# Local attention with two gated layers: a new order of the attention's instructions on each engine, and block means as three halves

## The chip, the cores and the metric

One core of a Trainium2 chip runs the whole program. The metric is the time of the program on the device in microseconds; three runs give a median, and one more run is profiled. TensorE is called PE here (PEld its weight loads), VectorE DVE, ScalarE ACT, GpSimd POOL, and SyncE SP, which issues all of this kernel's DMAs.

## The reference

Attention over 2 x 8 heads, 768 positions, head size 64. Each query sees the keys within 15 positions of it and, beside them, one summary for each of 24 blocks of 32 positions: the block's element-wise maximum of k and its mean of v. Two gated layers follow.

```
k_sum = k.reshape(B, H, nb, block, D).max(axis=3)
v_sum = v.reshape(B, H, nb, block, D).mean(axis=3)
scores_l = where(|pos_i - pos_j| < 16, scale * q k^T, -1e9)
scores_s = scale * einsum('bhsd,bhnd->bhsn', q, k_sum) + log(block)
a = exp(concat([scores_l, scores_s]) - max);  a = a / (sum(a) + 1e-9)
x = concat([v, v_sum]) weighted by a, heads side by side      # 1536 x 512
h = x @ w_in;   x = (h * cos(h)) @ w_out                      # d_ff 2048
h = x @ w_in2;  out = (h * tanh(softplus(h))) @ w_out2
```

## The kernel before

**Attention.** Heads are handled in 8 pairs, queries of a pair in 3 chunks of 256 positions (4 sub-blocks of 64), so there are NS = 24 chunks. The loop at L511 runs i = 0 to 28, and each pass ("turn") works on several chunks at different stages: scores and softmax of chunk i, transposes of the probabilities of chunk i-2 (`probsT`), their product with v of chunk i-3 (`pv`), and the split of the result of chunk i-4 into a high and a low part, `xh` and `xl` (`evac`), which are the layers' input. A turn also prepares later pairs: `prep_k` transposes k on PE, ACT copies it to `KX` (`ev`), DVE takes the block maxima `ks` (`kmax`), and POOL writes these into gaps of `KX` (`prep_ks`); `prep_q` transposes q, DVE scales it into `qt` (`qev`), POOL copies it into `QB` (`qbd`).

One sub-block's keys stand in one window of 118 rows or columns: 15 of the neighbour, 12 block summaries, 64 own, 12 block summaries, 15 of the other neighbour. `VW` holds these windows for v, three buffers, used in turn by the pairs. The block means of v in it come from two sources. For pairs 0 to 2, `prep_vm` multiplies `VW` by the constant `means` on PE (24 instructions) and ACT copies the result to `vm`. For pairs 3 to 7, `load_vb` loads the last 10 heads of v in two groups of 5 into one buffer `vb` (120 partitions of 8 KB), `block_sums` adds them up on POOL in 9 steps, and the means are `VS` (`vs`). `prep_vs` then spreads `vm` (4 DMAs) or `vs` (8 DMAs) over `VW`.

**Order of the work.** It is written out by hand. A phase name is given to each instruction by `at`; `flush` emits them phase by phase in the order of `ORDER` (L262), and each engine works through its own instructions strictly in that order. DMAs of `load`, `load_v` and `load_vb` are issued when the turn's plan is gone through, so ahead of all phases; those of `prep_vs` are in phase `misc`, at the end. SP's queue is in order as well: an issue that must wait for a buffer holds all that follow. Before, a turn's order is: on PE scores (L427 to L432), transposes of `pn`, preparing transposes, product with v; on DVE `mx` (L433), `qt`, the two instructions for `rs` (L441, L442), `xl`, `ks`; on ACT exponentials (L435), `xh`, `kx` and `vm`, `pt`; on POOL `pn` (L444), the copies to `QB`, the gaps of `KX`, the block sums.

**The first layer's weights.** They come as 64-bit numbers and are narrowed in place: `wnarrow` has one step on ACT (L131) and three on DVE (L135, L138, L141); `wsplit` makes a high part on ACT (L149) and a low part on POOL or DVE (L152). Chunks 0 to 3 are done in the attention by `filler(i)` (L524), which runs after all phases of turn i; it also has PE begin the first layer (`up`) at turns 24 to 26.

**Layers.** From L527 on: matrix products with operands split in high and low parts, gates on ACT and DVE, the narrowing of later weights on DVE. Nothing of them is changed.

Of the kernel before, what the change touches and what calls it, by code (L numbers as in the profile page):

```python
# [21 lines left out]
def kernel(  # L22
# [175 lines left out]
    def attention(filler):  # L198
        with ExitStack() as es:
# [11 lines left out]
            means = p1.tile([EXT, NSUB, NB], F32, tag="means", name="means")  # L211
# [37 lines left out]
            def build_means():  # L249

                nc.gpsimd.memset(means, 1.0 / BLK)
                for pattern, base, step in (
                    ([[SUB, NSUB], [-BLK, NB]], -SIDE, 1), ([[-SUB, NSUB], [BLK, NB]], SIDE + BLK - 1, -1),
                    ([[0, NSUB], [0, NB]], -SIDE, 1), ([[0, NSUB], [0, NB]], SIDE + SUB - 1, -1),
                ):
# [6 lines left out]
            ORDER = ("sc", "max", "exp", "tp", "tr", "qev", "rec", "norm", "xh", "xl", "ev", "pth", "kmax", "pv", "qbd", "misc")  # L262
# [38 lines left out]
            def block_sums(g, c):  # L301
# [4 lines left out]
                at("misc", nc.gpsimd.tensor_tensor, out=x[:, r:r + n, :], in0=x[:, r:r + n, :],  # L306
                   in1=x[:, r + w:r + w + n, :], op=ALU.add)
                if c == 8:
                    at("misc", nc.gpsimd.tensor_scalar, out=VS[g], in0=x[:, 0, :], scalar1=1.0 / BLK, scalar2=None,
                       op0=ALU.mult)  # L310

            def prep_vm(n):

                ps = BANK[4][0:NB, 256:384]
                for s in range(NSUB):
                    at("tr", nc.tensor.matmul, ps, lhsT=means[:, s, :], rhs=VW[n % 3][:, s], start=(s == 0),
                       stop=(s == NSUB - 1))
                vm = VM[n] = p2.tile([NB, 2, D], F32, tag="vm", name="vm")
                at("ev", nc.scalar.copy, vm.rearrange("p e d -> p (e d)"), ps)

            def prep_vs(n):

                for h in range(2):
                    for r0, s0 in ((HALO, h), (SIDE + SUB, 1 - h)):
                        dst = VW[n % 3][r0:r0 + GAP, s0:NSUB:2]
                        if 2 * n < MADE:
                            src = VM[n][GAP * h:GAP * h + GAP].rearrange("p e d -> p (e d)")
                            at("misc", nc.sync.dma_start, out=dst.rearrange("p s e d -> p s (e d)"),
                               in_=src[:, None, :].to_broadcast([GAP, NSUB // 2, 2 * D]))
                            continue  # L330
                        for e in range(2):
                            i = 2 * n + e - MADE
                            x0 = NB * (i % HPG) + GAP * h
                            at("misc", nc.sync.dma_start, out=dst[:, :, e, :],
                               in_=VS[i // HPG][x0:x0 + GAP, None, :].to_broadcast([GAP, NSUB // 2, D]))
# [7 lines left out]
            def prep_ks(n):  # L343
# [4 lines left out]
                for h in range(2):  # L348
                    at("misc", eng.tensor_copy, x[:, h:NSUB:2, 0:GAP],
                       ks[:, None, GAP * h:GAP * h + GAP].to_broadcast([128, NSUB // 2, GAP]))  # L350
                at("misc", eng.tensor_copy, KX[n % 2][:, HALO + NSUB * PITCH:HALO + NSUB * PITCH + GAP],
# [51 lines left out]
            for n in range(1, NP):  # L403
                if 2 * n < MADE:
                    plan(3 * n + 1, prep_vm, n)
                plan(3 * n + 2 if 2 * n < MADE else 3 * n, prep_vs, n)
                if n > 2:
                    plan(3 * n - 3, load_v, n)
            for g in range(2):
                plan((2, 7)[g], load_vb, g)  # L410
                for c in range(9):
                    plan((4, 10)[g] + c // 2, block_sums, g, c)
# [63 lines left out]
            wz = p1.tile([128, 512], BF16, tag="wz", name="wz")  # L476
            nc.vector.memset(wz, 0.0)

            def warm(m, bank):
                for _ in range(m):  # L480
# [468 lines left out]
```

## Time and profile before

| | us |
|---|---|
| median of 3 runs (lowest, highest) | 676.29 (675.84, 678.15) |
| profiled execution | 674.55 |
| its span, first to last instruction | 672.6 |
| PE busy, share of the span | 621.8, 92% |
| DVE busy | 503.1, 75% |
| ACT busy | 333.7, 50% |
| POOL busy | 87.0, 13% |

The span holds two parts. The attention takes the first 150 us or so, and there all engines are partly idle; in the layers PE is close to always busy. Busy shares over the whole span therefore say little of the attention: it has to be read by stretches, and in it turn by turn. A row of a timeline gives the start, the duration and, in brackets, how long the engine had been idle before it and which instruction ended that.

### The profile page before, as it was taken

The page shows a single profiled execution, that of the slowest core. Times are in us where ns is not written, and L with a number is a line of the kernel's source. Part 1 is how long each engine was busy: PE and PEld are TensorE (multiplying, and loading weights), DVE is VectorE, ACT ScalarE, POOL GpSimd, SP SyncE. Part 2 cuts the span into 40 slices and gives each one's busy share as a digit, 9 for nine tenths or more (in the row PEclk, how much of TensorE's full clock was granted, in tenths as well). Part 3 has the DMA queues.
Part 4 walks back from the last instruction along what each step waited for, and adds up shares of the span by engine and source line. Part 5 has one row for each costly group of instructions (what it writes and reads, how often), then busy time and mean ns, then how long its engine had stood idle before and what let it go on. Part 6 is the DMA issues. An engine that isn't in the chain of part 4 may idle for free.

```text
span 672.6 us, 8404 instructions
## 1 busy us (share of the span) xinstructions
PE 621.8 (92%) x2971; PEld 517.9 (77%) x2972; DVE 503.1 (75%) x879; ACT 333.7 (50%) x730; POOL 87.0 (13%) x160
## 2 busy tenths in 40 slices
PE   8782877788799999999999999999999999999998
PEld 5682766766588888888888888888888888888886
DVE  4453466639968898888888996887888888888654
ACT  3463366647655564444444555566343534444330
POOL 6373475410000000000000124000000000000000
PEclk9897879788899999999999999999999999999999
DMA  9856864101312231121121110021212121121004
GB/s 189 152 106 133 148 152 97 47 1 62 95 62 88 92 104 63 62 64 62 63 62 64 64 62 1 9 94 54 95 32 94 33 93 63 63 71 55 0 17 172
DMA packets 61207, 51.17 MB, mean 76 GB/s; under 512 B 48158, under 2 KB 49278, under 8 KB 60926
## 3 DMA queue, kind: packets, MB, share of 16 engines
q1 hardware_dynamic: 61166, 50.65, 28.4%
q8 instruction: 23, 0.38, 0.2%
q14 instruction: 18, 0.15, 0.1%
HBM read 46.31 MB, written 3.15 MB: 74 GB/s over the span
## 4 chain that ended last, share of the span: by engine, by line
PE 79%; ACT 7%; DVE 7%; POOL 2%; issue 2%; DMA 1%; SPq 0%; ACTq 0%; POOLq 0%; DVEq 0%
PE bank L706 19%; PE bank L577 19%; PE bank L691 18%; PE bank L188 18%; PE bank L266 5%; ACT pb L266 4%; DVE mx L266 2%; ACT xh L266 1%; DMA kn<-in_k_dram 1%; DVE wx L138 1%; ACT pt L266 1%; ACT kx L266 1%; DVE r L555 1%; DVE r L554 1%; DVE ks L266 1%
## 5 line engine op out<-in xcount | busy, mean ns | idle before, releaser
L188 PE MATMUL bank<-xh,ws 128*128 128x512 f32 x384 | 129.4, 399 | 2.0 <-DVE gg L561 1.9
L577 PE MATMUL bank<-gh,ws 128*128 128x512 f32 x384 | 126.3, 391 | 4.3 <-ACT ws L149 3.1
L706 PE MATMUL bank<-ws,gh 128*128 128x512 f32 (+1 forms) x388 | 118.5, 387 | 0.0
L691 PE MATMUL bank<-xh,ws 128*128 128x512 f32 x272 | 91.0, 389 | 0.0
L188 PEld LDWEIGHTS bank<-xh,ws 128*128 128x128 f32 x384 | 74.4, 194 | 18.5 <-DVE gg L561 2.8
L577 PEld LDWEIGHTS bank<-gh,ws 128*128 128x128 f32 x384 | 72.2, 188 | 20.6 <-ACT ws L149 3.7
L706 PEld LDWEIGHTS bank<-ws,gh 128*128 128x128 f32 x388 | 72.6, 188 | 14.9
L188 PE MATMUL bank<-xl,ws 128*128 128x512 f32 x192 | 76.6, 399 | 0.0
L553 ACT ACTIVATE n<-bank,b_quarter 128x512 int32<-128x512 f32 x48 | 32.9, 686 | 86.3 <-PE bank L188 86.3
L706 PE MATMUL bank<-ws,gl 128*128 128x512 f32 (+1 forms) x194 | 75.0, 387 | 0.0
L577 PE MATMUL bank<-gl,ws 128*128 128x512 f32 x192 | 74.7, 389 | 0.0
L149 ACT CAST ws<-wx 128x512 fp32r<-128x512 f32 x64 | 39.6, 620 | 51.5 <-DVE wx L141 51.5
L266 ACT ACTIVATE pb<-bank,mx 128x118 f32<-128x118 f32 x96 | 33.2, 358 | 55.6 <-DVE mx L266 49.6
L691 PEld LDWEIGHTS bank<-xh,ws 128*128 128x128 f32 x272 | 51.1, 188 | 10.6
L662 DVE TENSOR_TENSOR gl<-gg,gh 128x512 fp32r<-128x512 f32 x48 | 34.0, 708 | 30.2 <-ACT gh L661 30.2
L718 DVE TENSOR_TENSOR acc<-acc,bank 128x512 f32<-128x512 f32 (+1 forms) x71 | 47.5, 674 | 8.5 <-PE bank L706 8.5
L691 PE MATMUL bank<-xl,ws 128*128 128x512 f32 x136 | 52.9, 389 | 0.0
L554 DVE SCALAR_TENSOR_TENSOR r<-n,bank 128x512 f32<-128x512 int32 x48 | 32.9, 685 | 26.2 <-ACT n L553 26.1
L592 POOL TENSOR_TENSOR xl<-acc,xh 128x512 fp32r<-128x512 f32 x10 | 14.6, 1474 | 263.1 <-ACT xh L590 263.1
L266 PE MATMUL bank<-pt,vw 118*128 118x128 f32 x192 | 30.0, 306 | 18.3 <-DMA vw<-in_v_dram 12.7
L138 DVE SCALAR_TENSOR_TENSOR wx<-wst,wx 128x512 int32<-128x512 int32 x64 | 45.1, 705 | 2.2
L141 DVE SCALAR_TENSOR_TENSOR wx<-wst,wx 128x512 int32<-128x512 int32 x64 | 44.6, 697 | 1.8
(109 smaller groups left out, 1064.6 us busy)
## 6 DMA issues: line engine op xcount, KB each, us to landing
wst<-in_moe_w_in_dram SPq DMA_DIRECT2D x32, 512.0 KB
wst<-in_moe_w_out_dram SPq DMA_DIRECT2D x32, 512.0 KB
kn<-in_k_dram SPq DMA_DIRECT2D x16, 192.0 KB
qn<-in_q_dram SPq DMA_DIRECT2D x16, 192.0 KB
vw<-in_v_dram SPq DMA_DIRECT2D x16, 192.0 KB
out_dram<-acc SPq DMA_DIRECT2D x11, 256.0 KB
vb<-in_v_dram SPq DMA_DIRECT2D x2, 960.0 KB
vw<-in_v_dram SPq DMA_DIRECT2D x32, 41.2 KB
```

What stands on the lines that cost most here:

```text
L138: nc.vector.scalar_tensor_tensor(out=xi, in0=word[:, :, 0], scalar=29, in1=xi, op0=ALU.logical_shift_right, op1=ALU.bitwise_or)
L141: nc.vector.scalar_tensor_tensor(out=xi, in0=word[:, :, 1], scalar=-2 ** 31, in1=xi, op0=ALU.bitwise_and, op1=ALU.bitwise_or)
L149: nc.scalar.copy(hi, x)
L188: nc.tensor.matmul(ps, lhsT=SLOT[4 * (g % 2) + a][:, 512 * c + 128 * f:512 * c + 128 * f + 128], rhs=X[e][:, c, TB * j:TB * j + TB], start ...
L266: todo[phase].append(lambda: fn(*a, **kw))
L553: nc.scalar.activation(out=n, in_=h, func=AF.Identity, scale=1.0 / TWO_PI, bias=b_quarter)
L554: nc.vector.scalar_tensor_tensor(out=r, in0=n, scalar=-C1, in1=h, op0=ALU.mult, op1=ALU.add)
L577: nc.tensor.matmul(ps, lhsT=x, rhs=y, start=(n == 0), stop=(n == len(mm) - 1))
L662: later.append(lambda: nc.vector.tensor_tensor(out=lo, in0=g, in1=hi.bitcast(F32), op=ALU.subtract))
L691: nc.tensor.matmul(ps, lhsT=u, rhs=v, start=start and n == 0, stop=stop and n == len(mm) - 1)
L706: nc.tensor.matmul(ps, lhsT=x, rhs=y, start=(n == 0 and (h == 0 or not stay)), stop=(n == len(mm) - 1 and (h == NH - 1 or not stay)))
L718: nc.vector.tensor_tensor(out=acc, in0=acc, in1=ps, op=ALU.add)
```

## The change

`ORDER` is replaced: three new phases (`sums` for the block sums, `fill` for the weight work and `up`, `gap` for the gaps of `KX`) and another sequence. By engine, a turn is now: PE scores, preparing transposes (with the products for `vm`), transposes of `pn`, product with v, `up`; DVE `mx`, `qt`, weight steps, `ks`, `rs`, `xl`; ACT `xh`, `kx` and `vm`, `pt`, weight steps, exponentials; POOL block sums, weight halves, copies to `QB`, `pn`, gaps. `softmax`, which makes `rs` and `pn`, is called for chunk i-1 instead of i. `vm` becomes 12 partitions by three halves (first, second, first again), so that one DMA spreads two neighbouring halves over a row of windows: `prep_vs` has two DMAs a pair. For pairs 3 to 7, `vm` is now filled in turn 3n by four small DMAs from `vs` and a copy on POOL, and `prep_vs` follows in turn 3n+1. `means` holds 6 sub-blocks by 12 instead of 12 by 24 columns. The second `vb` load goes from turn 7 to 9 and its sums from 10 to 11 on; weight chunks 2 to 5 load one or two turns later. The warm-up products of PE have 256 columns, and there are twice as many.

```diff
-            ORDER = ("sc", "max", "exp", "tp", "tr", "qev", "rec", "norm", "xh", "xl", "ev", "pth", "kmax", "pv", "qbd", "misc")
+            ORDER = ("sc", "xh", "sums", "max", "tr", "tp", "ev", "qev", "pv", "pth", "fill", "qbd", "kmax", "rec", "exp",
+                     "xl", "norm", "gap", "misc")
...
             def prep_vm(n):
-                ps = BANK[4][0:NB, 256:384]
-                for s in range(NSUB):
-                    at("tr", nc.tensor.matmul, ps, lhsT=means[:, s, :], rhs=VW[n % 3][:, s], start=(s == 0),
-                       stop=(s == NSUB - 1))
-                vm = VM[n] = p2.tile([NB, 2, D], F32, tag="vm", name="vm")
-                at("ev", nc.scalar.copy, vm.rearrange("p e d -> p (e d)"), ps)
+                vm = VM[n] = p2.tile([GAP, 3, 2, D], F32, tag="vm", name="vm")
+                if 2 * n >= MADE:
+                    for e in range(2):
+                        i = 2 * n + e - MADE
+                        src = VS[i // HPG][NB * (i % HPG):NB * (i % HPG) + NB]
+                        for h in range(2):
+                            at("misc", nc.sync.dma_start, out=vm[:, h, e, :], in_=src[GAP * h:GAP * h + GAP])
+                    at("misc", nc.gpsimd.tensor_copy, vm[:, 2], vm[:, 0])
+                    return
+                for h in range(2):
+                    ps = BANK[4][0:GAP, 256 + 128 * h:384 + 128 * h]
+                    for s in range(NSUB // 2):
+                        at("tr", nc.tensor.matmul, ps, lhsT=means[:, s, :], rhs=VW[n % 3][:, NSUB // 2 * h + s],
+                           start=(s == 0), stop=(s == NSUB // 2 - 1))
+                ps = BANK[4][0:GAP, 256:512].rearrange("p (h e d) -> p h e d", h=2, e=2)
+                at("ev", nc.scalar.copy, vm[:, 0:2], ps)
+                at("ev", nc.scalar.copy, vm[:, 2], ps[:, 0])
 
             def prep_vs(n):
-
-                for h in range(2):
-                    for r0, s0 in ((HALO, h), (SIDE + SUB, 1 - h)):
-                        dst = VW[n % 3][r0:r0 + GAP, s0:NSUB:2]
-                        if 2 * n < MADE:
-                            src = VM[n][GAP * h:GAP * h + GAP].rearrange("p e d -> p (e d)")
-                            at("misc", nc.sync.dma_start, out=dst.rearrange("p s e d -> p s (e d)"),
-                               in_=src[:, None, :].to_broadcast([GAP, NSUB // 2, 2 * D]))
-                            continue
-                        for e in range(2):
-                            i = 2 * n + e - MADE
-                            x0 = NB * (i % HPG) + GAP * h
-                            at("misc", nc.sync.dma_start, out=dst[:, :, e, :],
-                               in_=VS[i // HPG][x0:x0 + GAP, None, :].to_broadcast([GAP, NSUB // 2, D]))
+                for h, r0 in ((0, HALO), (1, SIDE + SUB)):
+                    at("misc", nc.sync.dma_start,
+                       out=VW[n % 3][r0:r0 + GAP].rearrange("p (s h) e d -> p s (h e d)", h=2),
+                       in_=VM[n][:, h:h + 2].rearrange("p h e d -> p (h e d)")[:, None, :].to_broadcast(
+                           [GAP, NSUB // 2, 4 * D]))
...
             for n in range(1, NP):
-                if 2 * n < MADE:
-                    plan(3 * n + 1, prep_vm, n)
-                plan(3 * n + 2 if 2 * n < MADE else 3 * n, prep_vs, n)
+                plan(3 * n + 1 if 2 * n < MADE else 3 * n, prep_vm, n)
+                plan(3 * n + 2 if 2 * n < MADE else 3 * n + 1, prep_vs, n)
...
             for g in range(2):
-                plan((2, 7)[g], load_vb, g)
+                plan((2, 9)[g], load_vb, g)
                 for c in range(9):
-                    plan((4, 10)[g] + c // 2, block_sums, g, c)
+                    plan((4, 11)[g] + c // 2, block_sums, g, c)
...
                 if i < NS:
                     scores(i)
-                    softmax(i)
+                if 1 <= i < NS + 1:
+                    softmax(i - 1)
...
+                at("fill", filler, i)
                 flush()
-                filler(i)
...
-    for c, (t0, t1) in enumerate(((7, 10), (9, 12), (12, 15), (14, 17))):
+    for c, (t0, t1) in enumerate(((7, 10), (9, 12), (13, 16), (15, 18))):
...
-    at_step(17, wload, 0, 0, 4)
-    at_step(19, wload, 0, 0, 5)
+    at_step(19, wload, 0, 0, 4)
+    at_step(21, wload, 0, 0, 5)
```

In `block_sums` the phase is `sums` in place of `misc`, in `prep_ks` it is `gap`.

## Rows read from the trace of the kernel before

**Rows 1.** Busy time by stretch: us, busy (x count) by engine, clock, DMA share, GB/s.

```profile
40.00:52.50 12.50, 10.77 (x92) 9.75 (x91) 7.35 (x19) 7.77 (x33) 9.62 (x18) 1.00 0.37 79
56.40:68.40 12.00, 0.01 (x1) 0.04 (x1) 1.61 (x5) 2.37 (x10) 1.72 (x4) 0.64 1.01 206
86.00:94.00 8.00, 6.30 (x29) 5.98 (x30) 5.44 (x13) 5.20 (x17) 6.58 (x10) 0.57 0.31 67
152.70:176.30 23.60, 17.34 (x64) 12.45 (x62) 23.12 (x39) 15.97 (x26) 0.00 (x0) 0.92 0.28 89
176.30:672.60 496.30, 492.96 (x2173) 408.16 (x2173) 404.67 (x651) 237.29 (x398) 14.58 (x10) 1.00 0.20 64
```

**Rows 2.** SP's waits, up to 140 us: us in total, times, longest.

```profile
SPq L299 <- POOL vs L266: 12.3, 1, 12.3
```

**Rows 3.** Timeline of turn 9, SP and PE: start, us, instruction.

```profile
58.80 4.92 SPq L266 DMA_DIRECT2D vw<-vm  x4
68.39 2.05 PE L266 MATMUL bank<-pt,vw 118*128 118x128 f32 x8 [12.72 <-DMA vw<-in_v_dram]
```

**Rows 4.** Timeline of one turn without weight work, DVE and ACT.

```profile
41.38 0.64 DVE L266 TENSOR_REDUCE mx<-bank 128x4 f32<-128x472 f32 x1
42.11 0.36 ACT L266 ACTIVATE pb<-bank,mx 128x118 f32<-128x118 f32 x1 [1.11 <-DVE mx L266]
43.62 0.17 DVE L266 TENSOR_SCALAR rs<-sm 128x4 f32<-128x4 f32 x1 [1.27 <-ACT pb L266]
44.24 0.86 DVE L266 TENSOR_TENSOR xl<-bank,xh 64x256 fp32r<-64x256 f32 x2 [0.24 <-ACT xh L266]
44.50 0.59 ACT L266 COPY pt<-bank 118x512 f32<-118x512 f32 x1
45.47 0.64 DVE L266 TENSOR_REDUCE mx<-bank 128x4 f32<-128x472 f32 x1
```

**Rows 5.** Timeline, PE: the first instruction of turns 8 and 9.

```profile
49.70 0.36 PE L266 MATMUL bank<-mask,msel 67*128 67x472 bf16 x1
52.56 0.36 PE L266 MATMUL bank<-mask,msel 67*128 67x472 bf16 x1
```

**Rows 6.** Weight chunks in the attention: xcount, ns shortest/median/longest, first and last start.

```profile
L131 ACT ACTIVATE wx<-wst x4: 671/680/691, 76.2 to 113.4; 128x512 f32<-128x512 f32 x4
L135 DVE TENSOR_SCALAR wx<-wx x4: 427/672/1345, 76.9 to 114.1; 128x512 int32<-128x512 int32 x4
L138 DVE SCALAR_TENSOR_TENSOR wx<-wst,wx x4: 892/893/894, 81.5 to 119.6; 128x512 int32<-128x512 int32 x4
L141 DVE SCALAR_TENSOR_TENSOR wx<-wst,wx x4: 691/692/1099, 82.5 to 120.5; 128x512 int32<-128x512 int32 x4
L152 POOL TENSOR_TENSOR ws<-wx,ws x4: 1257/1268/1270, 89.7 to 126.2; 128x512 fp32r<-128x512 f32 x4
```

**Rows 7.** Timeline, PE: the scores of turn 3.

```profile
25.65 2.03 PE L266 MATMUL bank<-kx,qb 128*128 128x118 f32 x8 [4.18 <-POOL kx L266]
```

**Rows 8.** Timeline of SP's issues: v of one pair, then its means.

```profile
109.88 0.66 SPq L288 DMA_DIRECT2D vw<-in_v_dram  x1
113.54 6.68 SPq L266 DMA_DIRECT2D vw<-vs  x8
```

**Rows 9.** POOL's instructions, columns as in rows 6.

```profile
L266 POOL COPY qb<-qt x42: 388/396/549, 20.2 to 129.4; 64x256 f32<-64x256 f32 x42
L266 POOL TENSOR_TENSOR pn<-pb,rs x24: 971/972/974, 12.8 to 139.5; 128x472 f32<-128x472 f32 x24
L266 POOL TENSOR_TENSOR vb<-vb x18: 318/722/1173, 36.7 to 99.4; 120x256 f32<-120x256 f32 x14, 120x128 f32<-120x128 f32 x2, 120x64 f32<-120x64 f32 x2
```

**Rows 10.** Timeline of the attention's end, PE and DVE.

```profile
137.75 0.60 PE L266 MATMUL bank<-ident,pn 128*118 128x128 f32 x4
140.50 1.14 PE L266 MATMUL bank<-pt,vw 118*128 118x128 f32 x8 [2.15 <-ACT pt L266]
152.67 0.69 DVE L554 SCALAR_TENSOR_TENSOR r<-n,bank 128x512 f32<-128x512 int32 x1
```

More of the change, by code (lines that the diff above doesn't have):

```diff
@@ L210, in attention @@
             mask = p1.tile([MROWS, 6, EXT], BF16, tag="mask", name="mask")
-            means = p1.tile([EXT, NSUB, NB], F32, tag="means", name="means")
+            means = p1.tile([EXT, NSUB // 2, GAP], F32, tag="means", name="means")
             def build_mask():
@@ L252, in build_means @@
                 for pattern, base, step in (
-                    ([[SUB, NSUB], [-BLK, NB]], -SIDE, 1), ([[-SUB, NSUB], [BLK, NB]], SIDE + BLK - 1, -1),
-                    ([[0, NSUB], [0, NB]], -SIDE, 1), ([[0, NSUB], [0, NB]], SIDE + SUB - 1, -1),
+                    ([[SUB, NSUB // 2], [-BLK, GAP]], -SIDE, 1), ([[-SUB, NSUB // 2], [BLK, GAP]], SIDE + BLK - 1, -1),
+                    ([[0, NSUB // 2], [0, GAP]], -SIDE, 1), ([[0, NSUB // 2], [0, GAP]], SIDE + SUB - 1, -1),
                 ):
@@ L305, in block_sums @@
                            (0, 2, 2), (0, 1, 1))[c]
-                at("misc", nc.gpsimd.tensor_tensor, out=x[:, r:r + n, :], in0=x[:, r:r + n, :],
+                at("sums", nc.gpsimd.tensor_tensor, out=x[:, r:r + n, :], in0=x[:, r:r + n, :],
                    in1=x[:, r + w:r + w + n, :], op=ALU.add)
                 if c == 8:
-                    at("misc", nc.gpsimd.tensor_scalar, out=VS[g], in0=x[:, 0, :], scalar1=1.0 / BLK, scalar2=None,
+                    at("sums", nc.gpsimd.tensor_scalar, out=VS[g], in0=x[:, 0, :], scalar1=1.0 / BLK, scalar2=None,
@@ L348, in prep_ks @@
                 for h in range(2):
-                    at("misc", eng.tensor_copy, x[:, h:NSUB:2, 0:GAP],
+                    at("gap", eng.tensor_copy, x[:, h:NSUB:2, 0:GAP],
                        ks[:, None, GAP * h:GAP * h + GAP].to_broadcast([128, NSUB // 2, GAP]))
-                at("misc", eng.tensor_copy, KX[n % 2][:, HALO + NSUB * PITCH:HALO + NSUB * PITCH + GAP],
+                at("gap", eng.tensor_copy, KX[n % 2][:, HALO + NSUB * PITCH:HALO + NSUB * PITCH + GAP],
                    ks[:, 0:GAP])
@@ L475, in attention @@
             load(0, "q")
-            wz = p1.tile([128, 512], BF16, tag="wz", name="wz")
+            wz = p1.tile([128, 256], BF16, tag="wz", name="wz")
             nc.vector.memset(wz, 0.0)
             def warm(m, bank):
-                for _ in range(m):
-                    at("sc", nc.tensor.matmul, BANK[bank], lhsT=wz[:, 0:128], rhs=wz, start=True, stop=True)
+                for n in range(2 * m):
+                    at("sc", nc.tensor.matmul, BANK[bank][:, 256 * (n % 2):256 * (n % 2) + 256], lhsT=wz[:, 0:128], rhs=wz,
+                       start=True, stop=True)
             make_identity(nc, ident)
```

## Prediction

> **What bounds the kernel now.** I read first the stretches of busy time and clock [rows 1], then the waits, then single turns in the order of time. "Turn i" is pass i of the attention loop; PE starts it with the scores of chunk i. Three marks cut the execution: PE begins the scores of turn 9 at 52.56 us [rows 5], the transposes of turn 24 at 137.75, and VectorE (DVE) its first instruction of the layers at 152.67 [rows 10]. So A, up to turn 9, is 52.56; B, turns 9 to 23, 85.19; C, the attention's tail, 14.92; D, the layers, 672.6 - 152.67 = 519.93. Around the span lie 674.55 - 672.6 = 1.95 us; the median of the runs is 1.74 above the profiled one.
>
> In D, VectorE is busy 23.12 of the first 23.60 us, and PE 492.96 of the 496.30 after them [rows 1]. Nothing of that is changed, so D moves as a block: what A to C lose, the kernel loses.
>
> B has two faults. The first is one stall. The second load of `vb` is issued at turn 7 but must wait 12.3 us on SP's queue until GpSimd (POOL) has made the first `vs` [rows 2], which it does last in its turn. Behind it stand the copies of pair 2's means, issued only from 58.80; PE's product of turn 9 waits 12.72 us, until 68.39 [rows 3]. The second is the length of a turn. In a turn without weight work [rows 4] ScalarE (ACT) waits 1.11 us for the row maxima `mx`. From one `mx` to the next, 4.09 us, VectorE sits in front of the row sums' reciprocal for 1.27 us until the exponentials are done, then 0.24 us for `xh`, and only after both halves of `xl` and a block maximum comes the next `mx`, on which the next exponentials hang. VectorE's own work is 4.09 - 1.27 - 0.24 = 2.58; ACT's runs without a break from 42.11 to the end of `pt` at 45.09, 2.98; PE's turn at the full clock is 52.56 - 49.70 = 2.86 [rows 5]. None of the three needs 4.09.
>
> **The change part by part.** *Reciprocals a turn later, `mx` first after the scores, `xl` last.* The reciprocal now asks for exponentials that ended a turn ago, and the exponentials, last on ACT, ask for an `mx` that VectorE made early. The ring between VectorE and ACT opens, and the largest of 2.58, 2.98 and 2.86 sets the turn. With one handover of 0.24, the one seen before `xl`, I take 3.2 for a turn without weight work. Seven of B's turns are such (9, 14, 15, 20 to 23): 22.4.
>
> *Weight work inside the turn.* Each of four chunks takes two turns of VectorE (10 and 11, 12 and 13, 16 and 17, 18 and 19): 2 x 2.58, plus the three steps at medians of 0.67, 0.89 and 0.69, plus 0.68 in which the first step waits for ScalarE's part [rows 6]. Behind that wait stand now `kmax`, the reciprocals and `xl`, where before it stood at the end of the turn. That is 8.1 a pair, 32.4 for four. B without more is 54.8.
>
> *The `vb` load at turn 9, the sums first on POOL.* SP's 12.3 us go: turn 8 has finished `vs` by then, and pair 2's copies no longer stand behind the load. But what was late there is late elsewhere. At turn 9 SP issues q of pair 5, v of pair 4, then `vb` (120 x 8 KB, 0.98 MB), a weight chunk (0.52 MB), and only then the four new small copies `vs` to `vm`. Six issues of v take 113.54 - 109.88 = 3.66 us [rows 8], and can start only when pair 1's last product has freed its buffer, at the end of turn 8. Then 1.5 MB at 206 GB/s, the rate of the stretch in which the first stall sat [rows 1], are 7.3 us. After their last byte comes the landing: nothing shows a small copy alone; it is between 0 and the 4.67 us from the end of issue at 63.72 to 68.39 [rows 3], nearer the low end since that row had a queue in front, so 1. The copies land about 12 us after turn 9 begins.
>
> Who waits: the last POOL instruction of turn 9 copies half of `vm` and waits for them. On POOL stand behind it turn 10's q copies (0.40 each, two) and its product `pn` (0.97) [rows 9], which end at 13.8. PE wants this `pn` in turn 11, at 3.2 + 4.05 + 1.7 (scores and preparing transposes of that turn) = 8.95. So PE stands 4.9 us. Afterwards POOL lags: turns 11 to 14 carry two sums each (0.72), two q copies, `pn`, and twice a weight half (1.27) [rows 6, 9], about 4.5 at the most against VectorE's 4.05; I add 1 for it and 1 for the same copy at turn 15, where a weight chunk again precedes it. Together 7, bounds 0 (all landed early) and 15 (a landing at 17, all sums at their longest, 1.17).
>
> The Trainium skill, *DMA: Bandwidth & Descriptors*, section on the anatomy of one DMA, gives a fixed cost of about 2.0 us per DMA, mostly the write receipt, for the GpSimd path; it speaks against a path of two copies in a row. No row here shows a small copy alone. Taken here, the landing would be 2 instead of 1 and the sum 1 us more.
> The same skill, *GPSIMD Engine Reference*, section 1, says POOL shares its SBUF interfaces with VectorE when the latter has two SBUF inputs or a two-port mode. A denser VectorE would then lengthen the sums; the row's spread up to 1.17 agrees, and the bound above holds it.
>
> *Clock.* In 40 to 52.5 us PE had 1.0 granted with 10.77 of 12.5 busy; in the 12 us of idleness it fell (mean 0.64), and in 86 to 94, with 6.30 of 8 busy at the slower pace, it was 0.57 [rows 1]. The new turns leave PE as little idle time as the first of these; the 4.9 us stall may drop the clock for one or two turns. I add 1 (0 to 3). B is 54.8 + 7 + 1 = 62.8, against 85.19: -22.4.
>
> *Means as halves, two DMAs a pair.* A pair's eight copies cost SP 6.68 us of issue [rows 8]; two of the same kind, at 1.23 each (4.92 for four [rows 3]), and four small ones at no more than 0.84 (6.68 / 8) are 5.8. SP is not the bound in B; its relief is counted at nothing. If it were, it would be under 1 us a pair. For pairs 0 to 2 the products with `means` stay 24 instructions, now ahead of the transposes: nothing.
>
> *A.* In turn 2, PE waits 4.18 us for POOL's part of `kx` [rows 7], which came after the q copies and the turn's own `pn`. Now `pn` is that of the turn before and the reciprocal no longer stands between; half goes, -2. The plain turns 3, 5, 6 and 8 and the smaller `means` table: -1. Bounds 0 and -4.
>
> *C.* PE's product waits 2.15 us for `pt` [rows 10], since ACT copies it behind `xh`, behind the exponentials of the same turn. Now the exponentials are last: -2, bounds 0 and -4. *Warm-up in 256 columns, later weight chunks*: the same columns, and chunk 3 still done at turn 20 before the layers need it at 24; nothing, and a turn if the loads were late.
>
> **The sum.** A 49.6, B 62.8, C 12.9, D 519.9: 645.2, plus 1.95, is 647.1 for the profiled execution, -27.4. With 1.74, the median is 648.8.
>
> **The rivals.** *R1, the stall only moves.* The copy behind `vb` lands at 17 rather than 12, and the sums take 1.17: B +8, 657. For it: DMA engines are fully taken in such a stretch (share 1.01) [rows 1]. *R2, POOL never waits*: the small copies slip through; B -8, 641. *R3, the order buys nothing*: another ring keeps the turn where it is, and only the SP wait goes; A and C stay and B loses 12.72 less the 4.9 at turn 11: 676.3 - 7.8 = 668.5. Against it: no ring in the new order needs an answer within the same turn but `mx` to exponentials. *R4, PE at the lower level throughout B*: twice 2.86 in 15 turns is 85.8, so only A's and C's part is left: 676.3 - 5 + 0.6, 672. The stretch at 86 to 94 speaks for it, the one at 40 to 52.5 against.
> *R5, slower: every pair's copy on POOL waits, not the first alone.* The place is the last POOL instruction of turns 9, 12, 15, 18 and 21; `pn` follows 1.8 after the landing, PE needs some 1.5 for the rest of its turn, so a pair takes L + 3.3 where L is the landing. Five pairs equal before (85.19 and the 5 from A and C) at L = 14.7; at L = 17, B is 101.5 and the kernel 676.3 + 16.3 - 5 = 687.6. Against it: only turn 9 has 1.5 MB in front; the others have v and at most one chunk.
>
> **How the numbers follow.** Forecast 0.54 (642 to 655), R1 0.18, R2 0.12, R3 0.07, R4 0.04, R5 0.05. Low end 636: R2 with A and C at their best. High end 665: B at +15 with A or C at nothing; it leaves out R3 to R5, 0.16, and a little at the low side. 0.3% (2 us) is about what can be told from no change. Faster: all but R5 and a part of R4, 0.94; same 0.01; slower 0.05.
>
> **What would show it.** SP's wait before `vb` gone; `mx` no longer behind `xl` and reciprocals free of waits; turns near 3.2 without and 4.05 with weight work; about 5 us of PE idle near turn 11, ended by POOL's `pn`, with a DMA wait on POOL before it; the stretch from the first layer instruction to the end still 520. It is wrong if turns stay at 4.1, if PE's clock stays low through B, or if POOL waits for DMA in every pair.

## The result, and the profile after

The changed kernel takes 655.17 us (653.64 to 655.38); beside it on the same chip the kernel before took 676.07 (675.36 to 678.15). The ratio is 0.968, with a 95% interval of 0.966 to 0.971. So it is faster, by about 21 us. The forecast was 648.8, 27.5 less than the median shown of before, with a range of 636 to 665.

The changed kernel cut at the same four marks (scores of turn 9, transposes of turn 24, first layer instruction on DVE), columns as in [rows 1]: busy us and count of PE, PE's loads, DVE, ACT, POOL, then clock, DMA share, GB/s.

```profile
0.00:48.76 48.76, 42.09 (x344) 36.70 (x345) 24.63 (x67) 27.39 (x108) 29.19 (x82) 1.00 0.92 177
48.76:121.75 72.99, 52.57 (x364) 48.72 (x361) 44.88 (x114) 47.71 (x191) 41.91 (x73) 0.84 0.54 119
121.75:132.73 10.98, 10.98 (x65) 9.58 (x66) 3.72 (x11) 5.23 (x15) 0.97 (x1) 1.00 0.00 0
132.73:653.50 520.77, 510.61 (x2237) 420.24 (x2235) 427.62 (x689) 253.13 (x423) 14.01 (x10) 0.99 0.20 65
```

| stretch | before | forecast | after |
|---|---|---|---|
| A | 52.56 | 49.6 | 48.76 |
| B | 85.19 | 62.8 | 72.99 |
| C | 14.92 | 12.9 | 10.98 |
| D | 519.93 | 519.9 | 520.77 |

A, C and D came within 2 us of their terms, A and C better. All that is missing is in B: 10.2 us.

The ring between VectorE and ScalarE did open. VectorE in turn 9 and the start of turn 10 of the changed kernel (start, us, instruction, idle before):

```profile
50.04 0.65 DVE L267 TENSOR_REDUCE mx<-bank 128x4 f32<-128x472 f32 x1
50.61 0.41 DVE L267 TENSOR_SCALAR qt<-bank 128x256 f32<-128x256 f32 x1
51.12 0.42 DVE L267 TENSOR_REDUCE ks<-bank 128x8 f32<-128x256 f32 x1
51.58 0.38 DVE L267 TENSOR_SCALAR rs<-sm 128x4 f32<-128x4 f32 x1
51.99 0.18 DVE L267 RECIPROCAL rs<-rs 128x4 f32<-128x4 f32 x1
52.09 0.83 DVE L267 TENSOR_TENSOR xl<-bank,xh 64x256 fp32r<-64x256 f32 x2
53.24 0.65 DVE L267 TENSOR_REDUCE mx<-bank 128x4 f32<-128x472 f32 x1 [0.33 <-PE bank L267]
```

Where [rows 4] had 1.27 in front of `rs` and 0.24 in front of `xl`, there is no wait but 0.33 for PE: 53.24 - 50.04 = 3.20, the number forecast. But few turns of B are like it. Turn lengths after, from one `mx` to the next, against the forecast:

| turns | forecast | after |
|---|---|---|
| 9, 14 | 3.2 each | 3.2, 3.1 |
| 10 + 11, with the stall | 8.1 + 4.9 | 3.95 + 12.45 |
| 12 + 13 | 8.1 (+1 POOL lag) | 5.06 + 5.18 |
| 15 | 3.2 + 1 | 6.60 |
| 16 + 17 | 8.1 | 4.32 + 3.89 |
| 18 + 19 | 8.1 | 5.30 + 4.64 |
| 20, 21, 22 | 3.2 each | 2.63, 6.64, 2.50 |

Turns 10 and 11 are 3.4 us over the forecast, turns 12 to 22 together 7.5 (49.8 against 42.3).

Some of the waits of the changed kernel up to 125 us (engine, tile, line, what it waited for: us in total, times, longest):

```profile
DVE mx L267 <- PE bank L267: 33.3, 17, 8.7
PE bank L267 <- POOL pn L267: 19.1, 12, 8.3
POOL vm L267 <- DMA vm<-vs: 12.6, 2, 9.5
DVE wx L135 <- ACT wx L131: 6.0, 4, 1.9
POOL ws L152 <- ACT ws L149: 5.8, 4, 2.0
PE bank L267 <- DVE rs L267: 2.2, 2, 1.1
```

The wait of [rows 2] is gone. `mx` still waits, but for PE's scores and no longer behind VectorE's own `xl`: VectorE is early now, and PE is what it waits for. PE in turn waits for `pn`, 19.1 us in twelve places. The largest is the one predicted; SP, POOL and PE around it:

```profile
48.95 1.39 SPq L289 DMA_DIRECT2D vw<-in_v_dram  x1
53.31 0.41 SPq L291 DMA_DIRECT2D vw<-in_v_dram  x1
53.81 0.36 SPq L300 DMA_DIRECT2D vb<-in_v_dram  x1
54.66 3.20 SPq L267 DMA_DIRECT2D vm<-vs  x4
62.78 0.28 POOL L267 COPY vm<-vm 12x128 f32<-12x128 f32 x1 [9.46 <-DMA vm<-vs]
64.96 1.11 PE L267 MATMUL bank<-ident,pn 128*118 128x128 f32 x4 [8.32 <-POOL pn L267]
```

and the DMA engines from 56 to 66 us in 40 slices of 0.25 us (busy tenths, and GB/s):

```profile
DMA  9999979999985889979872000000000000575366
GB/s 393 328 197 213 197 197 279 279 246 213 279 180 115 164 180 197 213 229 344 360 284 73 4 0 0 0 0 0 0 0 0 0 0 12 78 86 61 70 94 74
```

The bytes queued ahead are through at 61.5, the copy on POOL starts 1.3 later, and PE had stood since 64.96 - 8.32 = 56.64.

### The profile page after: what moved, and what is told of

Its sections match the earlier page's. It is cut to its first block, busy times and chain, and to the rows that moved or that the text cites. A ratio compares the mean times of both kernels' runs of the same rounds, so it can differ in the third digit from the quotient of the medians.

```text
span 653.5 us, 8522 instructions
## 1 busy us (share of the span) xinstructions
PE 616.2 (94%) x3004; PEld 515.2 (79%) x3004; DVE 500.9 (77%) x879; ACT 333.5 (51%) x733; POOL 86.1 (13%) x165
## 4 chain that ended last, share of the span: by engine, by line
PE 83%; DVE 6%; POOL 3%; DMA 3%; issue 1%; ACT 1%; SPq 1%; POOLq 0%; ACTq 0%; DVEq 0%
PE bank L709 20%; PE bank L580 20%; PE bank L694 19%; PE bank L188 18%; PE bank L267 7%; POOL pn L267 1%; DMA vb<-in_v_dram 1%; DMA vm<-vs 1%; DVE wx L138 1%; POOL qb L267 1%; DVE wx L141 1%; DVE r L558 1%; POOL ws L152 1%; DVE r L557 1%; DMA vw<-in_v_dram 1%
## 5 line engine op out<-in xcount | busy, mean ns | idle before, releaser
L138 DVE SCALAR_TENSOR_TENSOR wx<-wst,wx 128x512 int32<-128x512 int32 x64 | 45.6, 712 | 2.2
L141 DVE SCALAR_TENSOR_TENSOR wx<-wst,wx 128x512 int32<-128x512 int32 x64 | 44.4, 694 | 1.8
L152 DVE TENSOR_TENSOR ws<-wx,ws 128x512 fp32r<-128x512 f32 x60 | 42.1, 703 | 4.8 <-ACT ws L149 4.1
L671 ACT ACTIVATE gg<-gg 128x512 f32<-128x512 f32 x28 | 17.7, 633 | 51.2 <-DVE gg L670 51.2
```

The costliest lines, as they stand in the source:

```text
L138: nc.vector.scalar_tensor_tensor(out=xi, in0=word[:, :, 0], scalar=29, in1=xi, op0=ALU.logical_shift_right, op1=ALU.bitwise_or)
L141: nc.vector.scalar_tensor_tensor(out=xi, in0=word[:, :, 1], scalar=-2 ** 31, in1=xi, op0=ALU.bitwise_and, op1=ALU.bitwise_or)
L152: eng.tensor_tensor(out=lo, in0=x, in1=hi.bitcast(F32), op=ALU.subtract)
```

## The experiments

Every run has its ratio to the kernel before on the same chip. Differences of ratios below are turned into us at 676; each interval is about ±0.0025, 1.7 us, so a difference between two kernels of less than some 2.5 us says little.

| kernel | median us | ratio, interval | clock 50 to 115 us |
|---|---|---|---|
| changed kernel | 655.17 | 0.9681 (0.9655 to 0.9707) | 0.83 |
| b1_only_vb_later | 661.71 | 0.9777 (0.9755 to 0.9799) | 0.95 |
| m1_old_means | 650.68 | 0.9629 (0.9607 to 0.9651) | 0.89 |
| v1_vb_behind | 652.68 | 0.9644 (0.9621 to 0.9666) | 0.87 |
| v2_no_pool_copy | 651.83 | 0.9625 (0.9598 to 0.9653) | 0.87 |
| k1_kmax_rec_first | 652.79 | 0.9647 (0.9625 to 0.9669) | 0.89 |
| k2_pool_half_last | 650.60 | 0.9623 (0.9596 to 0.9650) | 0.92 |
| w1_filled_waits | 652.45 | 0.9661 (0.9636 to 0.9686) | 0.95 |
| c1_all_three | 648.82 | 0.9600 (0.9580 to 0.9619) | 0.89 |
| s1_old_means_sums_last | 653.22 | 0.9666 (0.9641 to 0.9691) | 0.88 |
| f1_best | 648.78 | 0.9612 (0.9580 to 0.9644) | 0.87 |
| f2_best_filled | 651.34 | 0.9639 (0.9612 to 0.9665) | 0.87 |
| h1_vb_early | 648.11 | 0.9584 (0.9558 to 0.9611) | 0.89 |

**What each part of the change is worth.** First the kernel before with nothing but the second `vb` load and its sums later (the sums in four turns instead of five):

```diff
-                plan((2, 7)[g], load_vb, g)
+                plan((2, 9)[g], load_vb, g)
-                    plan((4, 10)[g] + c // 2, block_sums, g, c)
+                    plan((4, 11)[g] + min(c // 2, (4, 3)[g]), block_sums, g, c)
```

> The kernel before with one part of the change alone: the second vb load at turn 9, its sums from turn 11 on (in four turns instead of five, so that they end by turn 14). Order, means and the rest are those of before. If SP's wait of 12.3 us was worth its whole length: about 663 to 664, and the new order gives the other 8 to 9 us of the 21. If the order does most and the stall only moves: above 670. If everything comes from the load: 655.

0.9777: 15 us less than before. Turn 9, 17.47 us from `mx` to `mx` before, takes 4.09, 13.4 less; the other turns keep their 4.1 and 5.7. So one stall is worth 13 to 15 us, a little more than the 12.72 of [rows 3], and the other 6 us or so come from the order and the rest of the change.

Then the changed kernel with `means`, `prep_vm` and `prep_vs` of before (`vm` of 24 rows, four or eight copies a pair straight into `VW`):

```diff
-                plan(3 * n + 1 if 2 * n < MADE else 3 * n, prep_vm, n)
-                plan(3 * n + 2 if 2 * n < MADE else 3 * n + 1, prep_vs, n)
+                if 2 * n < MADE:
+                    plan(3 * n + 1, prep_vm, n)
+                plan(3 * n + 2 if 2 * n < MADE else 3 * n, prep_vs, n)
```

> The changed kernel with the means as before the change: one table of 12 by 24 columns, eight DMAs a pair straight from vs into the windows in turn 3n, no small copies and no copy on POOL. Order and vb load stay changed. Theory Q (the chain small copies, POOL, two DMAs is the price): POOL's wait of 9.46 us and PE's 8.32 us at turn 11 go; the eight DMAs land behind vb and the weights, so the product of turn 12 may wait about 2 us: 647 to 650 against 655.2. Theory T (turns are long by themselves): 653 to 655. If eight issues of 6.7 us a pair make SP the bound: above 656.

0.9629: with the old means the kernel is 3.5 us faster than with the new. Of the 21.6 us (1 - 0.9681 of 676), 15 come from the load, 10 from the order with what else came along (later weights, warm-up; no run tells these apart), and the means as halves take 3.5 back. They cut both ways: with the old means `mx` of turn 9 comes at 51.64 instead of 50.04, so early on the halves save 1.6 us, and what they cost comes later. The stall does not go with the old means; it moves. POOL and PE of this kernel in turns 11 and 12:

```profile
64.02 1.40 POOL L267 TENSOR_TENSOR vb<-vb 120x256 f32<-120x256 f32 x2 [4.42 <-DMA vb<-in_v_dram]
67.32 1.11 PE L267 MATMUL bank<-ident,pn 128*118 128x128 f32 x4 [5.10 <-POOL pn L267]
```

The sums, now first on POOL, wait for the load itself, with `pn` behind them.

**The stall at turn 11.** Two kernels take one of the two causes away. In the first, the `vb` load goes behind the small copies:

```diff
-                nc.sync.dma_start(out=x, in_=src[r0:r0 + HPG * NB])
+                at("misc", nc.sync.dma_start, out=x, in_=src[r0:r0 + HPG * NB])
```

> The changed kernel with one edit: the second load of vb is issued behind the four small copies of turn 9 instead of ahead of the v load's end. Theory Q (the queue): in the changed kernel POOL's copy at turn 9 waits 9.46 us because the small copies stand behind 0.98 MB of vb and 0.52 MB of weights; PE then stands 8.32 us at turn 11. Without vb in front the copies land some 4 us earlier, POOL's wait falls to 5 to 6 us, PE's idle time to about 4, and the kernel to about 651.5 from 655.2. Theory T (the turn): what the changed kernel lacks against the forecast comes from turns that are too long by themselves (weight steps ahead of the block maxima, POOL's sums), so shortening the wait is given back by the next turns: 654 to 656.

In the second, no engine waits for the small copies: the third half comes by two more DMAs instead of the copy on POOL.

```diff
-                        for h in range(2):
-                            at("misc", nc.sync.dma_start, out=vm[:, h, e, :], in_=src[GAP * h:GAP * h + GAP])
-                    at("misc", nc.gpsimd.tensor_copy, vm[:, 2], vm[:, 0])
+                        for h in range(3):
+                            at("misc", nc.sync.dma_start, out=vm[:, h, e, :],
+                               in_=src[GAP * (h % 2):GAP * (h % 2) + GAP])
```

> The changed kernel with POOL's copy of the third half of vm replaced by two more small DMAs, so that POOL waits for no DMA of the means. Theory Q1: the wait on POOL is the price, since pn of the next turn stands behind it; without it 8.3 us go at turn 11 and up to 2 at turn 15: 645 to 648. Theory Q2: the means land when they land; the product of turn 12 then waits for them, at about 67 us where it ran at 70.3, so only 3 us go: 652, and PE's long wait is put down to the DMA of the means instead of POOL's pn. Theory T: 655.

0.9644 and 0.9625. In the first, turn 11 falls from 12.45 to 9.04, but turn 12 grows from 5.06 to 7.37. In the second, turn 11 is 3.83 as if nothing had been there, and turn 12 becomes 11.24:

```profile
61.63 1.41 POOL L267 TENSOR_TENSOR vb<-vb 120x256 f32<-120x256 f32 x2 [3.43 <-DMA vb<-in_v_dram]
63.89 1.74 SPq L267 DMA_DIRECT2D vw<-vm  x2
64.93 1.11 PE L267 MATMUL bank<-ident,pn 128*118 128x128 f32 x4 [4.10 <-POOL pn L267]
68.23 2.05 PE L267 MATMUL bank<-pt,vw 118*128 118x128 f32 x8 [2.19 <-DMA kn<-in_k_dram]
```

Twice more PE stands for the same load: once behind the sums, once for the windows' copies (the row names k, but the product reads `vw`, whose copies were issued up to 65.63). So the copy on POOL was only the first of three things behind the 0.98 MB; removing it uncovers the next, and brings 2 to 4 us of the 8.3. The time is that of theory Q2 of v2_no_pool_copy, 652; the wait behind the sums it had not seen. Turn 15, where pair 4's means are due, even grows with it, from 6.60 to 8.84.

**The turns without a stall.** Two edits of the order:

```diff
-            ORDER = ("sc", "xh", "sums", "max", "tr", "tp", "ev", "qev", "pv", "pth", "fill", "qbd", "kmax", "rec", "exp",
+            ORDER = ("sc", "xh", "sums", "max", "tr", "tp", "ev", "qev", "pv", "pth", "kmax", "rec", "fill", "qbd", "exp",
```

> The changed kernel with the block maxima and the reciprocals ahead of the weight steps on VectorE (nothing else moves, since only VectorE has work in these two phases). Theory T: in the changed kernel the k transposes of turns 13 and 19 wait 1.1 us each for the block maxima of the turn before, which stand behind a weight step that waits for ScalarE, and pn comes late by the same way; these waits go, each turn with weight work gains 0.5 to 1: 649 to 652. Theory Q: the turn's length there is POOL's or the clock's, the time stays within 1 us of 655.2.

```diff
-            eng.tensor_tensor(out=lo, in0=x, in1=hi.bitcast(F32), op=ALU.subtract)
+            step = lambda: eng.tensor_tensor(out=lo, in0=x, in1=hi.bitcast(F32), op=ALU.subtract)
+            if eng is nc.gpsimd:
+                LATE.append(step)
...
-                     "xl", "norm", "gap", "misc")
+                     "xl", "norm", "gap", "lo", "misc")
...
+                at("lo", late)
```

> The changed kernel with POOL's low half of a weight chunk as the last of its turn instead of ahead of the q copies and pn. Theory P: in the changed kernel this half waits for ScalarE's high half (5.8 us in all), pn stands behind it, and PE waits 2.0 to 2.5 us for pn in turns 15 and 21; these waits shrink and the turns around them by 2 us each: 650 to 652. Rival: the same wait of POOL falls on the next turn's instructions instead, 655.

0.9647 and 0.9623. What the first removes, in the changed kernel at 72 to 74 us (VectorE, then PE):

```profile
72.28 1.02 DVE L135 TENSOR_SCALAR wx<-wx 128x512 int32<-128x512 int32 x1 [1.66 <-ACT wx L131]
73.78 0.41 PE L267 MATMUL bank<-ident,kn 128*128 128x128 f32 x2 [1.10 <-DVE rs L267]
```

The weight step waits for ScalarE; the block maximum behind it reads the bank into which PE transposes the next k, so VectorE's wait reaches PE. (The row names `rs`; the maximum ended just before it.) With the maxima and reciprocals ahead, PE's waits for `rs`, 2.2 us, are gone, but those for `pn` grow from 19.1 to 22.1. The kernel takes 2.3 us less, on the edge of what can be told; where they come from is shown under the clock.

What the second removes, in the changed kernel at turn 20 (ScalarE, POOL, PE):

```profile
108.91 0.62 ACT L149 CAST ws<-wx 128x512 fp32r<-128x512 f32 x1
109.61 1.27 POOL L152 TENSOR_TENSOR ws<-wx,ws 128x512 fp32r<-128x512 f32 x1 [1.76 <-ACT ws L149]
111.74 1.90 POOL L267 TENSOR_TENSOR pn<-pb,rs 128x472 f32<-128x472 f32 x2
112.77 0.65 PE L267 MATMUL bank<-ident,pn 128*118 128x128 f32 x4 [2.46 <-POOL pn L267]
```

POOL waits 1.76 us for ScalarE's part of the chunk, which ScalarE itself does late in its turn; `pn` stands behind it. With POOL's half last in the turn, turns 15 and 21 go from 6.60 and 6.64 to 3.56 and 2.46; turns 16 and 17 grow by 2.5 together, and the kernel gains 3.9 us.

Turn 15 is not quite the same case. POOL and PE of the changed kernel there:

```profile
82.22 1.27 POOL L152 TENSOR_TENSOR ws<-wx,ws 128x512 fp32r<-128x512 f32 x1 [0.27 <-ACT ws L149]
85.39 0.65 PE L267 MATMUL bank<-ident,pn 128*118 128x128 f32 x4 [2.03 <-POOL pn L267]
87.63 1.90 PE L267 MATMUL bank<-kx,qb 128*128 128x118 f32 x8
```

Here POOL waits only 0.27 us for ScalarE; what stands ahead of `pn` is work, two block sums (1.25) and the half itself (1.27). And PE's wait of 2.03 is not all: the scores after it take 1.90 us, where they took 1.05 at 81.89, before the wait. Turn 15 falls to 3.55 in k1_kmax_rec_first as well, which leaves POOL's half in its place; PE waits 1.36 us there, and its clock stays at 1.00.

**The clock.** Six products of 256 columns, of no use to the result, ahead of the transposes of `pn`:

```diff
+                if 10 <= i < 24:
+                    for n in range(6):
+                        at("wm", nc.tensor.matmul, BANK[2 + i % 2][:, 256 * (n % 2):256 * (n % 2) + 256],
+                           lhsT=wz[:, 0:128], rhs=wz, start=True, stop=True)
```

> The changed kernel with six more warm-up products of 256 columns in each of turns 10 to 23, on PE ahead of the transposes of pn, where PE waits; their results are written over and not used. Theory C (the clock): in the changed kernel the mean granted clock from turn 9 to 24 is 0.84, where the earlier stretch of close turns has 1.00, because PE's idle time comes in one piece ahead of these transposes; filled, the clock holds, and 3 to 5 us go: 650 to 652. Theory P and Q (PE waits for others, its clock is not on the path): 655, or up to 6 us more where PE has no wait to fill, 14 turns by six products of 0.11 us being 9 us at most.

Three stretches of the changed kernel (columns as above, the clock is third from the end):

```profile
76.00:80.00 4.00, 3.83 (x19) 3.48 (x18) 3.89 (x8) 2.56 (x12) 2.60 (x5) 0.57 0.76 196
104.00:108.00 4.00, 4.00 (x25) 3.88 (x24) 3.12 (x9) 2.56 (x11) 3.13 (x6) 0.66 0.81 222
112.00:116.00 4.00, 3.23 (x18) 3.12 (x19) 0.63 (x2) 2.48 (x11) 1.87 (x3) 0.70 0.24 34
```

From the row maxima of turn 12 to those of turn 23, the same columns for the changed kernel, k1_kmax_rec_first, k2_pool_half_last and the filled kernel, and six of the added products:

```profile
69.64:119.49 49.85, 38.83 (x267) 35.98 (x266) 32.89 (x82) 34.30 (x135) 30.98 (x53) 0.86 0.47 106
69.80:116.76 46.96, 35.19 (x266) 32.93 (x265) 35.48 (x82) 34.26 (x135) 30.59 (x53) 0.93 0.51 113
69.60:114.41 44.81, 34.28 (x267) 31.27 (x266) 32.82 (x81) 33.90 (x132) 31.45 (x54) 0.96 0.58 119
69.02:117.33 48.31, 39.74 (x333) 36.03 (x332) 32.94 (x81) 34.29 (x135) 31.84 (x54) 1.00 0.54 112
56.91 0.82 PE L267 MATMUL bank<-wz 128*128 128x256 bf16 x6
```

Filled, the clock is 1.00 in these turns, 0.95 over 50 to 115 us; the time is 0.9661 against 0.9681, within the intervals. The 66 added products of these turns take about 9 us at 0.82 for six (an estimate), so the rest of PE's work took some 30.7 us, where the changed kernel's took 38.83; yet the stretch is only 1.5 us shorter, as PE spent the difference on the products. The clock's worth alone is not isolated by this. f2_best_filled, below, comes out 1.8 us the other way, without a higher clock.

The lines of k1_kmax_rec_first and k2_pool_half_last say more. PE's idle time hardly changes in them: 11.0 us in the changed kernel (49.85 - 38.83), 11.8 and 10.5 in these two. The same 267 instructions (266 in one trace) keep PE busy for 38.83, 35.19 and 34.28 us. So what the two edits gave back in these turns, 2.9 and 5.0 us, is in the traces PE's pace and not less waiting. Which waits bring the clock down does not come out of the rows: it fell behind those of 2.03 and 2.46 us in turns 15 and 21, but in k1_kmax_rec_first it stayed at 1.00 behind one of 2.23 at 100.5 us.

**All together.** The old means with both edits of the order:

> Three edits of the changed kernel together: means as before, maxima and reciprocals ahead of the weight steps, POOL's weight half last. If the three causes stand beside one another: 655.2 less about 6, 2.4 and 4: 642 to 644. If they hide one another: 646 to 649.

0.9600: 5.5 us less than the changed kernel, where the three alone add up to 9.7. PE's waits for `pn` are down from 19.1 to 8.9 us, but turn 18 grows to 8.53: PE waits there 5.1 us. The row names a load of v, but v of pair 5, which this product reads, was issued by 71.6; the last of the pair's eight copies of means was issued up to 93.80, and the product runs at 95.45. The rest of the runs ask where the load and its sums may stand. First the old means alone again, with the sums last on POOL:

```diff
-            ORDER = ("sc", "xh", "sums", "max", "tr", "tp", "ev", "qev", "pv", "pth", "fill", "qbd", "kmax", "rec", "exp",
-                     "xl", "norm", "gap", "misc")
+            ORDER = ("sc", "xh", "max", "tr", "tp", "ev", "qev", "pv", "pth", "fill", "qbd", "kmax", "rec", "exp",
+                     "xl", "norm", "gap", "sums", "misc")
...
-                    plan((4, 11)[g] + c // 2, block_sums, g, c)
+                    plan((4, 11)[g] + 4 * c // 9, block_sums, g, c)
```

> The changed kernel with the means of before, and the block sums last on POOL instead of first. With the means of before alone POOL stood 4.4 us in front of the first sum of the second group, waiting for the load of vb, with the product pn behind it, and PE stood 5.1 us behind that. Theory: this wait is the price of putting the sums first; with the sums behind pn it hits nobody, and the 650.7 us become about 646, with no wait of PE for pn above 1.5 us in turns 11 to 13. Rival: the load's bytes hold the queue anyway, and the wait goes to the product of turn 12, which needs pair 3's means: 650 to 651.

0.9666: 2.5 us more than m1_old_means, where some 5 less were expected, and more than the rival gave. POOL waits 0.16 for `vb` now, but the rival's wait is there: the product of turn 12 stands for pair 3's windows, whose last copies are issued only at 64.72 (the row names `pb`, which the product does not read; it reads `pt` and `vw`):

```profile
64.72 2.16 SPq L267 DMA_DIRECT2D vw<-vs  x2
68.55 2.05 PE L267 MATMUL bank<-pt,vw 118*128 118x128 f32 x8 [3.25 <-ACT pb L267]
```

That alone would still be a gain: turns 11 to 13 take 16.4 us together, against 18.4 with the sums first. What is longer lies elsewhere: `mx` of turn 9 comes 1.2 us later (52.79), and turn 18 takes 9.14 instead of 6.74, with PE standing 3.9 us until pair 5's copies, issued up to 96.31, have landed.

The next kernel has the edits of v2, k1 and k2, the sums last and the load of v1, and moves load and sums once more:

```diff
-                plan((2, 9)[g], load_vb, g)
-                    plan((4, 11)[g] + c // 2, block_sums, g, c)
+                plan((2, 10)[g], load_vb, g)
+                    plan(4 + 4 * c // 9 if g == 0 else 13 + c // 5, block_sums, g, c)
```

> The changed kernel with what the runs so far found to help: six small transfers into vm instead of four and a copy on POOL, block maxima and reciprocals ahead of the weight steps, POOL's half of the weights last, the sums last, and the second load of vb issued at the end of turn 10, its sums from turn 13 on. If the gains were independent, 655.2 less 3.3, 2.4, 4.6 and 2.5 would be 642; they overlapped before (three gave 6.4), so 641 to 647, the middle 644. Rival: the 0.98 MB of vb hold something of pair 3 or 4 wherever they are put, and it stays at 648 to 650.

The same with four filling products a turn:

> The kernel before this one with four products of 256 columns, of no use to the result, ahead of the transposes of pn in turns 10 to 23. Theory: what is left in the attention is PE's granted clock, which falls in turns with idle time; filled, the clock of 50 to 115 us is 0.95 or more and the time 1 to 3 us less. Rival: there is no clock left to gain, and the 56 products at about 0.11 us each cost up to 6 us.

And the first again with the load two turns earlier:

```diff
-                plan((2, 10)[g], load_vb, g)
-                    plan(4 + 4 * c // 9 if g == 0 else 13 + c // 5, block_sums, g, c)
+                plan((2, 8)[g], load_vb, g)
+                    plan(4 + c // 3 if g == 0 else 11 + 4 * c // 9, block_sums, g, c)
```

> The kernel with all edits together, but group 0's sums packed into turns 4 to 6, so that the second load of vb can go out at the end of turn 8, behind pair 2's copies, without waiting for the buffer; its sums run in turns 11 to 14. In the kernel with all edits together the load stood at the end of turn 10 and pair 4's means came 6.3 us late at turn 16, while the DMA engines moved only 17 to 74 GB/s around the end of turn 7. Theory: what is left of the stall is where the 0.98 MB of vb fall; put into that gap they delay nobody, and 648.8 becomes 641 to 645. Rival: the burst then stands in front of v of pair 4 and pair 3's means, PE waits for them at turns 11 to 13 instead, and it stays at 647 to 651.

0.9612, 0.9639 and 0.9584. The first and the last stay at the rivals' times, 648 to 650 and 647 to 651; the filling brings nothing there, and the clock over 50 to 115 us is 0.87 with it as without. With the load at turn 10, pair 4's means come late: PE stands 6.3 us in turn 15. With it at turn 8, pair 3's do. SP and PE of this last kernel:

```profile
47.02 0.48 SPq L277 DMA_DIRECT2D vb<-in_v_dram  x1
50.02 4.15 SPq L300 DMA_DIRECT2D vw<-in_v_dram  x1
58.13 4.71 SPq L277 DMA_DIRECT2D vm<-vs  x6
63.33 1.74 SPq L277 DMA_DIRECT2D vw<-vm  x2
67.60 2.05 PE L277 MATMUL bank<-pt,vw 118*128 118x128 f32 x8 [6.86 <-DMA vw<-vm]
```

and its DMA engines from 58 to 68 us, in slices of 0.25 us:

```profile
DMA  1649889895300001000000000004663567699999
GB/s 23 137 80 188 208 299 311 360 442 199 101 4 7 5 0 38 7 0 6 6 0 4 8 0 0 0 0 74 74 78 62 86 78 80 118 209 289 238 264 244
```

Here PE stands while the DMA engines carry next to nothing: from 60.75 to 64.75 at most 38 GB/s. It is not the bytes any more. SP's issue of one copy of v stood 4.15 us (0.64 for the next of its kind, at 55.37), so everything behind it is late; then six small copies cost 4.71 of issue and two spreading ones 1.74; and the last of these lands 67.60 - 65.07 = 2.5 us after its issue has ended.

The best of these, h1_vb_early, beats the changed kernel by 6.6 us (0.9584 against 0.9681), and c1_all_three, with an interval that overlaps it, by 5.5. Both still have PE idle for over 5 us in one place. A second buffer for `vb`, which would uncouple the load from the first sums, was not tried; whether its 8 KB a partition fit beside the attention's tiles was not looked at.

## Why the prediction was right, and where it was short

**The sign and the mechanism held.** SP's wait is gone, `rs` waits for exponentials only once up to 125 us, 0.9 us, where before it did in 19 places for 21.8 in all, `mx` no longer waits for VectorE's own work but for PE (0.33 us in turn 9, 33.3 in all), the plain turn is 3.2 and 3.1 in turns 9 and 14, one large stall stands at turn 11, ended by `pn`, with a DMA wait on POOL before it, and D is 520.8. The range held the time. The forecast's own bounds, 642 to 655, just missed it: the time lies 6.4 us above the forecast and within 2 of R1's 657, though not by R1's way, as the next paragraph shows.

**The term of turn 11 was mis-sized: PE's wait was forecast at 4.9 and measured at 8.3**, each step a little. The landing was 14.0 us after the turn's start (62.78 - 48.76), not 12: the six issues of v took 4.8 from 48.95, not 3.66; the bytes 7.8 from there, not 7.3; and the landing after them 1.3, not 1. That the four copies of 3 KB were not done before the big load agrees with the Trainium skill (*DMA: Bandwidth & Descriptors*, section on queues, rings and completion order): the write that reports a transfer lands only after every earlier write of that DMA engine. The fixed cost of about 2.0 us that the Trainium skill gives for DMAs issued by GpSimd (same page, anatomy of one DMA) is not what a small copy issued by SP took: on nearly idle engines, in h1_vb_early, SP goes on 0.5 us after the sixth small copy's issue ended (62.84 to 63.33). The spreading copies there took 2.5. The other 1.4 us: PE came to its wait at 7.9 rather than 8.95, and `pn` followed the landing by 2.2 instead of 1.8. Of R1, the landing was nearer the forecast's 12 than its 17, and the sums did not lengthen at all (longest 0.73, where it had 1.17): not R1, but the forecast's own step at a larger size. Other instructions did lengthen side by side, though, which the forecast took at their medians: the weight step L138 took 1.97 us beside two sums at 75.71 (0.69 in the other chunks), and two q copies 1.72 beside L138 and L141 at 104.12 (0.85 in most turns).

**One term was missing: what POOL and VectorE carry in front of `pn` and `ks`.** The prediction added up POOL's work in turns 11 to 14 (4.5 against 4.05) as if POOL never waited, gave 1 us for it, and counted turns 14 and 20 as plain, though POOL has its half of a chunk to do in them. In fact that half waits for ScalarE, 1.77, 0.27, 1.98 and 1.76 us in turns 12, 14, 18 and 20, and `pn` stands behind the wait and the half. PE then stood 2.0 and 2.5 us in turns 15 and 21, which took 6.6 instead of 4.2 and 3.2, and moving the half gave back 3.9 us (k2_pool_half_last). The prediction named what is queued behind VectorE's wait of 0.68, but not that PE's bank hangs on it; the wait itself was 1.7 and 1.9 in two of the four places, and moving the maxima ahead gave 2.3 (k1_kmax_rec_first). Both are the same slip: a wait that costs nothing at the end of a turn was moved inside one, and only its length was counted, not who waits behind it.

**The means as halves were costed at nothing, and cost 3.5** (m1_old_means; 1.6 saved up to turn 9, some 5 lost after it). The sentence "SP is not the bound in B" was read from shares. On the path from `vs` to the product, what counts is SP's time of issue and two landings in a row, and this path set a turn in the changed kernel, in v2_no_pool_copy, f1_best and h1_vb_early.

**The clock: 1 us forecast, and too little.** B's mean is 0.84, hardly above before's 0.82, so the reading of the 40 to 52.5 us stretch as typical of B was wrong: PE is idle for 20.4 of B's 73 us, and behind some of its waits the stretches have 0.57 to 0.70. In turns 12 to 22, which are 7.5 us over the forecast, the same instructions keep PE busy 38.83 us at 0.86 and 34.28 at 0.96 (k2_pool_half_last): 4.6 of the 5.0 us that this edit gave back there. In the traces, then, what this edit gave back lies in PE's pace after the waits, and hardly in their length. R4's clock, then, was there in part. What the clock alone is worth was not isolated: filling with products brought 0.9661 instead of 0.9681, within the intervals, and in f2_best_filled the clock did not rise.

**A and C were better than forecast.** PE's wait for `kx`, which stands ahead of the scores of turn 3, fell from 4.18 [rows 7] to 1.61, and the halves of the means save some 1.6 by turn 9. In C the wait for `pt` [rows 10] is gone, and PE is busy for all of its 10.98 us at a clock of 1.00 (0.89 before); the forecast had counted the wait but not the clock.

## What to carry to other kernels

When a wait is moved from the end of a turn into it, list what stands behind it on that engine and which of it another engine needs next; the price is paid there, and not in the length of the wait. When an edit has paid, compare PE's busy time for the same instructions before and after, not its waits alone: in two of the edits here the gain lay there. A large transfer in an in-order queue is paid by whatever is next needed from that queue: taking away the waiter only shows the next one, so find a place for the transfer where nothing behind it is due for as long as it takes, and count the issue time and landing of each copy in a chain.

## What the runs showed of the hardware

After the issue of a 0.98 MB load, SP took three more loads and then stood in the middle of an issue. It could be seen in the kernel before already, at the first load, in turn 2 (the issue of q ends at 32.57, 7.36 after 25.21):

```profile
25.21 0.54 SPq L299 DMA_DIRECT2D vb<-in_v_dram  x1
26.94 5.63 SPq L279 DMA_DIRECT2D qn<-in_q_dram  x2
```

At the second load of h1_vb_early it is 7.15 (47.02 to 54.17). At the second load of the changed kernel, which a weight chunk and four small copies follow, there is no such stand. What fills up there, no run shows.

A spreading copy of 72 KB took 2.5 us from the end of its issue to the product that waited for it (h1_vb_early), although the engines had been nearly idle before; one of 18 KB took 1.7 (c1_all_three at 95.45, s1_old_means_sums_last at 98.00).

Instructions of VectorE and POOL that ran side by side could slow one another: the weight step L138 took 1.97 us beside two block sums, and 0.69 in the changed kernel otherwise.
